# Replaying a fixed instruction order, banks and evacuating engines in place of a greedy planner: attention with memory, gated feed-forward, one core

## The chip, the cores and the metric

The kernel runs on one core of one Trainium2 chip. Five engines work side by side: TensorE (PE in the profile, its weight loads PEld), VectorE (DVE), ScalarE (ACT), GpSimd (POOL) and SyncE (SP), which here only issues DMAs. Each engine carries out its own instructions in order and waits on semaphores for those of the others. The metric is the device time of one launch in microseconds; lower is better.

## The reference

Two branches are computed from the same 2048 x 512 input and mixed per token by a sigmoid gate. Branch A is attention with 32 heads of width 16 in four segments of 512 tokens, plus a read of a running memory M, z of the segments before. Branch B is a feed-forward block of width 1792 with a ReLU gate. Cut to what matters:

```python
for s in range(4):
    logits = einsum('bhqd,bhkd->bhqk', qs, ks) * scale + mask   # causal inside the segment
    a_dot = einsum('bhqk,bhkd->bhqd', softmax(logits), vs)
    num = einsum('bhld,bhde->bhle', phi(qs), M)
    den = einsum('bhld,bhd->bhl', phi(qs), z)[..., None] + 1e-06
    outs.append(g * num / den + (1.0 - g) * a_dot)              # g = sigmoid(beta), per head
    M = M + einsum('bhld,bhle->bhde', phi(ks), vs)
    z = z + einsum('bhld->bhd', phi(ks))
a = concat(outs) @ wo
b = (relu(x @ W_gate) * (x @ W_up)) @ W_down
out = sig * a + (1 - sig) * b                                   # sig = sigmoid(sum(x * gate_w))
```

All inputs and the output are bfloat16.

## The kernel before

The kernel is a small planner and an emitter. `program` (from L619 on) walks through the computation and makes one `Op` for each group of instructions: its engine or engines, its code, the names that it reads and writes, and for work in PSUM an `Epoch`, the holder of a bank. `Sched.add` numbers the operations and works out what each depends on. `Sched.run` then places them one by one with a model of their durations, `Sched.place` notes which semaphores each has to wait for, and `Sched.emit` writes the five engines' programs. Nothing of the planning is left at run time: what the chip sees are five fixed instruction lists with waits.

The work of each segment s:

- **Projections** (`proj`). q and k by head group of 128 columns (four groups G), v by token tile: 16 products each of 128 x 128 weights on 512 columns. An evacuation casts each PSUM bank to SBUF (`qcp`, `kcp`, `vcp`; DVE or ACT), and two masks of k (`kmask`) write `kp`, in which the two heads of a pair stand apart. For the first segment's q, `step = 1 if early else 2` makes every product an operation of its own, and the list is then put in order by contraction tile.
- **Attention** (`att`). 18 visits: `visit` makes a "quad" (L912), four row tiles of 32 that fill four PSUM banks at once, an exponential over 2048 columns on ACT (L928) into `E`, and on POOL the causal masks (L934). After the visits of a head group, `flush` makes its PV block (L968, 64 matmuls on two banks), two transposes on DVE that empty the banks (`tr`, L978), and a chain `rden`, `rdg`, `ad`, `bt`, `oa` that divides, scales and turns the result into `oT`.
- **Memory** (`mu`, `nd`): an update of M (L835) and, from the second segment on, four readouts (L855).
- **Feed-forward** (`ffn`): 14 blocks f, each with 4 products for gate and 4 for up (L1042), a ReLU (`relu`, DVE or ACT) and a product with it (`hm`, DVE) into `hT`.
- **Output** (`outp`): per token tile 4 products with wo (L1074) and 14 with W_down (L1081) in one bank, a final scaling (`fin`) and a store. The last tile is split into 384 and 128 columns.
- **Gate** (`gate`): rows of x are loaded again (`ldxr`, L742) into the slots `osb`, multiplied and summed on DVE (L745). From the second segment on all rows use slot 2.

The x of the first segment is loaded plainly (`ldhT`) and turned by PE against the identity (L706, `xt`), with eight copies (`xc`) on DVE and ACT. Ahead of it PE runs warm-up products on constants (L692). The weights follow on SP, all loads of the first half of gate and up (`ldwg0`, `ldwu0`), then the second half (`ldwg1`, `ldwu1`).

The order is made greedily: for each engine there are queues with priorities; `ready` says from when an operation may start by the model, `_choose` takes one, with a jitter and other settings drawn from a seed for every 8 us of planned time; `_bank_choice` picks PSUM banks, 0 to 3 for the visits and mostly 4 to 7 for the rest; an evacuation that may run on DVE or ACT goes to whichever takes it first. `DCOST`, `LAND0` and `landing` say how long loads take.

Of the kernel before, what the change touches and what calls it, by code (L numbers as in the profile page):

```python
# [2 lines left out]

# [13 lines left out]
LAG = 0  # L17
PAIR = 1
LASTK = 17
HWAIT = 250.0  # L20
HEARLY = 3500.0
MWAIT = 500.0
PVR = 2
NEXT = 1150.0
TNN = 2
STRICT = 6000.0
PE_LAT = 175.0
SWITCH = 106.0
GATE_T = {0: 20000.0, 1: 44000.0, 2: 90000.0, 3: 140000.0}
UNIT_T = 400.0  # L30
X1_T = 19000.0
X2_T = 34000.0
H1_T = 14000.0
LX = 300.0
DCOST = {"ldwg0_0": 1000.0, "ldbraw": 1800.0, "ldgwb": 1300.0, "ldx1_0": 1500.0, "vsh0": 1100.0, "vsh1": 1100.0, "vsh2": 1100.0, "vsh3": 1100.0}
LAND0 = {"ldhT0": 2850.0, "ldhT2": 3100.0, "ldwq0": 3150.0, "ldwq1": 3200.0, "ldwq2": 3100.0, "ldwq3": 3000.0}
NBLK = 36
QTN, EKN, HTN, OTN, XR = 8, 4, 19, 8, 3
SBX = 0
LOW_T = {"main": 0.0, "att": 3000.0, "proj": 2000.0, "ffn": 2000.0, "mid": 3000.0, "out": 5000.0}  # L40
WIN = 8000.0
EVAC_P = 0.5
ND_P = 0.2
ADP = 1
TSP = 0
OAP = 0
UNITS = [[8] * 18] * 4
ORDER = [[(0, 1, 7, 2, 6, 3, 5, 4), (4, 0, 1, 7, 2, 6, 3, 5)] * 2] * 4
# [30 lines left out]
class Epoch:  # L79
    _n = 0  # L80

    def __init__(self, cls="mid", nb=1, at=None):
        self.nb = nb
        self.at = at
        self.group = (self,)
        Epoch._n += 1
        self.res = f"ACCep{Epoch._n}"
        self.bank = None
        self.readers = []
        self.cls = cls  # L90


class Op:
    __slots__ = ("engs", "eng", "fns", "occs", "lat", "reads", "writes", "name", "dma", "nbytes", "mode", "ep", "role",
                 "after", "nbk", "port", "base", "preds", "stream", "idx", "start", "end", "done", "cidx", "gate", "nd", "mates")

    def __init__(self, alts, reads=(), writes=(), name="", lat=0.0, dma=False, nbytes=0, mode="f", ep=None, role=None):
# [13 lines left out]
        self.after = 0.0  # L111
        self.nbk = 2
        self.port = name.startswith(PORT)
        self.base = None
        self.preds = []
        self.gate = None
        self.mates = ()
# [11 lines left out]
class Sched:  # L129
    ENGS = ("pe", "act", "dve", "pool", "sp")  # L130
    CAPS = {"ffn": 3, "proj": 2, "mid": 2, "out": 2}

    def __init__(self, ndma=16, nbanks=8, seeds=(0,)):
        self.seeds = seeds
        self.jit = {}
        self.knobs = {}
        self.low_from = False
        self.mates = ()
# [9 lines left out]
        self.queues = {e: [] for e in self.ENGS}  # L148
        self.dma_rr = 0
        self.port_free = 0.0  # L150
        self.relax = False
# [7 lines left out]
        self.busy = {e: 0.0 for e in self.ENGS}  # L159
        self.ops = []  # L160
        self.log = []
# [8 lines left out]
    def add(self, op):  # L170
# [42 lines left out]
        self.ops.append(op)  # L213
        return op

    def queue(self, prio, ops):
        by = {}
        for t in ops:
            for e in t.engs:
                by.setdefault(e, []).append(t)  # L220
        for e, ts in by.items():
            self.queues[e].append([prio, ts, 0])

    def _bank_free(self, prev, e):
        if prev is None:
            return 0.0
        return max((r.end + LAT for r in prev.readers if self.know[e][r.stream] < r.idx), default=0.0)

    def pv_due(self):
        q = self.queues["pe"][self.pvq]  # L230
        while q[2] < len(q[1]) and q[1][q[2]].done:
            q[2] += 1
        if q[2] >= len(q[1]) or q[1][q[2]].gate is None:
            return 0
        t = self.now["pe"] + 500.0
        return (PVR if q[1][q[2]].mates else q[1][q[2]].nbk) if all(p.done and p.end <= t for p, _ in q[1][q[2]].preds) else 0

    def next_visit(self):
        q = self.queues["pe"][self.attq]
        while q[2] < len(q[1]) and q[1][q[2]].done:  # L240
            q[2] += 1
        return q[1][q[2]] if q[2] < len(q[1]) else None

    def visit_in(self, dt):
        op = self.next_visit()
        if op is None:
            return False
        t = self.now["pe"] + dt
        if op.after > t or not all(p.done and p.end <= t for p, _ in op.preds):
            return False  # L250
        return all(p.done and p.end <= t + 700.0 for g in op.ep.group for rd in g.readers for p, _ in rd.preds if p.ep not in op.ep.group and p.cidx < op.cidx)

    def soon(self, dt):
        op = self.next_visit()
        if op is None or op.after - HEARLY > self.now["pe"] + dt:
            return False
        if not all(p.done and p.end + LAT <= self.now["pe"] + dt for p, _ in op.preds):
            return False
        t = max((self._bank_free(x, "pe") if x is None or all(r.done for r in x.readers) else 1e9) for x in self.bank_ep[:4])
        return t <= self.now["pe"] + dt  # L260

    def next_sides(self):
        op = self.next_visit()
        return 0 if op is None else len(op.ep.group) - 1

    def low(self, cls):
        return 0 if self.low_from and (self.relax or not self.visit_in(LOW_T[cls])) else 4

    def _bank_choice(self, ep, e, taken=()):
        cls, nb, n = ep.cls, ep.nb, len(self.bank_ep)  # L270
        idle = [i not in taken and (p is None or all(r.done for r in p.readers)) for i, p in enumerate(self.bank_ep)]
        if ep.at is not None:
            own = range(ep.at, ep.at + nb)
            return (ep.at, max(self._bank_free(self.bank_ep[i], e) for i in own)) if all(idle[i] for i in own) else None
        lo = 4 if cls == "side" else self.low(cls)
        if cls in ("proj", "ffn", "mid", "out"):
            held = sum(not f and p.cls == cls for f, p in zip(idle, self.bank_ep))
            if held + nb > (self.knob()[3] if cls == "ffn" else 2):
                return None
            free = sum(idle[lo:])  # L280
            if (free - nb < max(self.pv_due(), 1) if nb == 1 else free < (2 if self.relax else 3)):
                return None
            room = sum(idle[4:]) - (self.next_sides() if self.visit_in(self.knob()[1]) and not self.relax else 0)
        else:
            room = 8
        best = None
        for bi in range(lo, n - nb + 1):
            if not all(idle[bi:bi + nb]) or bi + nb > 4 and min(nb, bi + nb - 4) > room:
                continue
            ft = max(self._bank_free(p, e) for p in self.bank_ep[bi:bi + nb])  # L290
            key = ft + (300.0 if bi < 4 else 0.0)
            if nb == 1:
                key += 0.0 if not idle[bi ^ 1] else 200.0
            if best is None or key < best[2]:
                best = (bi, ft, key)
        return best and best[:2]

    def _banks(self, op, e):
        taken, out, t = set(), [], 0.0
        for ep in op.ep.group:  # L300
            bc = self._bank_choice(ep, e, taken)
            if bc is None:
                return None
            out.append((ep, bc[0]))
            taken |= set(range(bc[0], bc[0] + ep.nb))
            t = max(t, bc[1])
        return out, t

    def _pred_done(self, op, e):
# [5 lines left out]
    def ready(self, op, e):  # L315
        t0 = self.now[e]
        t = op.after - (HEARLY if op.mode == "r" and self.mode == "h" else 0.0)
        if op.gate is not None:
            if self.mode != "r" and not self.relax and not (op.gate.done and self.now["pe"] > op.gate.start + STRICT) and not (op.gate.done and (self.next_visit() is None or self.soon(NEXT))):
                return None  # L320
            for m in op.mates:
                for p in self._pred_done(m, e):
                    if p.eng != "pe":
                        if not p.done:
                            return None
                        t = max(t, p.end + LAT - 900.0)
            lo = self.low("att")
            ft = sorted(self._bank_free(p, e) for p in self.bank_ep[lo:] if p is None or all(r.done for r in p.readers))
            if len(ft) < op.nbk:
                return None  # L330
            t = max(t, ft[op.nbk - 1])
        for p in self._pred_done(op, e):
            if not p.done:
                return None
            if self.know[e][p.stream] < p.idx:
                t = max(t, p.end + LAT)
        if op.ep is not None:
            if op.role == "w" and op.ep.bank is None:
                for rd in [x for g in op.ep.group for x in g.readers]:
                    for p, _ in rd.preds:  # L340
                        if p.ep in op.ep.group or p.cidx > op.cidx:
                            continue
# [121 lines left out]
    def _choose(self, e):  # L464
# [28 lines left out]
        if not heads:  # L493
            return None
# [707 lines left out]
```

## Time and profile before

| | us |
|---|---|
| median of 3 runs | 263.42 |
| lowest, highest | 262.78, 263.67 |
| profiled execution, its own time | 263.54 |
| its span, first to last instruction | 262.3 |

The profile page says for each engine how long it was busy; the view of the chain follows the work back from the last instruction and names what each step waited for. A row of a timeline begins with its start and its length in us; in rows of groups the number behind the bar is the busy time in us and then the mean length of one in ns. A PE row's length includes the drain of the array, so consecutive matmuls overlap: the distance of two starts is what one costs.

### The profile page before, as it was taken

What the parts mean: (1) busy time and instruction counts of PE and PEld (TensorE: products, weight loads), DVE (VectorE), ACT (ScalarE), POOL (GpSimd) and SP (SyncE); (2) the same over time, 40 slices, a digit from 0 to 9 for tenths busy, and PEclk for the clock granted to TensorE, in tenths of its full rate; (3) what the DMA queues carried; (4) which work ended last, traced back from release to release, by engine and by line L of the source; (5) the groups of instructions that cost most, each with busy time, mean ns of one, the idle gap of its engine ahead of it and who ended that gap; (6) DMA issues with size and microseconds to landing.
All of it is one profiled execution on the core that took longest, in us unless ns stands there. A gap on an engine that the chain in (4) does not pass through costs nothing.

```text
span 262.3 us, 6420 instructions
## 1 busy us (share of the span) xinstructions
PE 255.7 (97%) x2619; PEld 114.7 (44%) x2653; DVE 179.5 (68%) x356; ACT 184.5 (70%) x160; POOL 130.7 (50%) x295
## 2 busy tenths in 40 slices
PE   8999999999999999999999999999999999999997
PEld 5444443444344544434444544444444444444444
DVE  5488878788986577778788577757667716467600
ACT  4586689999789779785778687677777665576021
POOL 3036557564646457666645457846364454545100
PEclk9999999999999999999999999999999999999999
DMA  6999746930261135212040232010132100100011
GB/s 200 290 308 249 162 63 135 287 46 22 66 143 40 24 74 109 62 23 24 19 107 7 56 96 27 2 41 2 22 82 43 23 21 22 40 2 2 0 42 40
DMA packets 34925, 19.87 MB, mean 76 GB/s; under 512 B 24016, under 2 KB 34128, under 8 KB 34896
## 3 DMA queue, kind: packets, MB, share of 16 engines
q1 hardware_dynamic: 34800, 19.46, 31.6%
q8 instruction: 21, 0.34, 0.6%
q14 instruction: 8, 0.07, 0.1%
q10 hardware_dynamic: 96, 0.00, 0.0%
HBM read 10.40 MB, written 2.11 MB: 48 GB/s over the span
## 4 chain that ended last, share of the span: by engine, by line
PE 97%; issue 1%; DVE 1%
PE ps L1042 38%; PE ps L1081 19%; PE ps L792 11%; PE ps L912 9%; PE ps L968 6%; PE ps L790 5%; PE ps L1074 5%; PE ps L855 1%; PE ps L692 1%; PE ps L706 1%; PE ps L835 0%; DVE hT L1053 0%; DVE Tn L978 0%; DVE osb L745 0%; DVE osb L1090 0%
## 5 line engine op out<-in xcount | busy, mean ns | idle before, releaser
L934 POOL TENSOR_SCALAR_AFFINE_SELECT E<-E 64x256 bf16<-64x256 bf16 (+1 forms) x256 | 110.3, 442 | 112.2 <-ACT E L928 82.9
L928 ACT ACTIVATE E<-ps 128x2048 bf16<-128x2048 f32 x72 | 135.1, 1876 | 38.7 <-PE ps L912 38.6
L1042 PE MATMUL ps<-xT,wu 128*128 128x512 bf16 x213 | 57.2, 380 | 1.4 <-issue 1.3
L1042 PE MATMUL ps<-xT,wg 128*128 128x512 bf16 x219 | 57.7, 380 | 0.6 <-issue 0.3
L1081 PE MATMUL ps<-wd,hT 128*128 128x512 bf16 (+2 forms) x229 | 52.8, 367 | 0.9 <-issue 0.6
L1053 DVE TENSOR_TENSOR hT<-ps,rl 128x512 bf16<-128x512 f32 x56 | 38.5, 687 | 16.6 <-PE ps L1042 16.4
L1081 PEld LDWEIGHTS ps<-wd,hT 128*128 128x128 bf16 x238 | 21.4, 98 | 23.8 <-issue 2.4
L1042 PEld LDWEIGHTS ps<-xT,wg 128*128 128x128 bf16 x224 | 20.6, 98 | 25.7 <-issue 2.8
L1042 PEld LDWEIGHTS ps<-xT,wu 128*128 128x128 bf16 x224 | 20.1, 98 | 25.4 <-issue 3.5
L912 PE MATMUL ps<-qT,kp 32*128 32x192 bf16 (+7 forms) x512 | 28.6, 287 | 0.0
L978 DVE STREAM_TRANSPOSE Tn<-ps 128x512 f32<-128x512 f32 x32 | 21.3, 696 | 8.7 <-PE ps L968 8.7
L1051 DVE TENSOR_SCALAR rl<-ps 128x512 bf16<-128x512 f32 x30 | 20.7, 690 | 8.5 <-PE ps L1042 8.2
L1090 DVE TENSOR_SCALAR osb<-ps,omg 128x512 bf16<-128x512 f32 (+1 forms) x8 | 5.6, 701 | 26.0 <-PE ps L1081 15.1
L1050 ACT ACTIVATE rl<-ps 128x512 bf16<-128x512 f32 x26 | 15.5, 598 | 10.0 <-PE ps L1042 9.7
L912 PEld LDWEIGHTS ps<-qT,kp 32*128 32x128 bf16 x512 | 8.2, 92 | 25.3 <-issue 13.1
L968 PE MATMUL ps<-E,vaug 64*17 64x128 bf16 (+7 forms) x512 | 18.7, 283 | 0.0
L968 PE MATMUL ps<-E,vsh 64*17 64x128 bf16 (+7 forms) x512 | 18.3, 283 | 0.0
L1091 ACT ACTIVATE osb<-ps,omg 128x512 bf16<-128x512 f32 (+1 forms) x9 | 6.1, 674 | 16.4 <-PE ps L1074 14.0
L792 PE MATMUL ps<-xT,wq 128*128 128x512 bf16 x61 | 16.0, 390 | 0.4 <-issue 0.3
L1074 PE MATMUL ps<-wo,oT 128*128 128x512 bf16 (+2 forms) x67 | 16.2, 366 | 0.2 <-issue 0.2
L792 PE MATMUL ps<-xT,wk 128*128 128x512 bf16 x60 | 15.6, 380 | 0.4 <-issue 0.3
L968 PEld LDWEIGHTS ps<-E,vaug 64*17 64x17 bf16 x512 | 11.6, 86 | 8.5 <-issue 4.4
(68 smaller groups left out, 233.6 us busy)
## 6 DMA issues: line engine op xcount, KB each, us to landing
vsh<-vaug SPq DMA_DIRECT2D x8, 272.0 KB, 4.2
osb<-in_A_x_dram SPq DMA_DIRECT2D x16, 128.0 KB, 2.3
out_dram<-osb SPq DMA_DIRECT2D x15, 128.0 KB, 1.7
wg<-in_B_W_gate_dram SPq DMA_DIRECT2D x8, 224.0 KB, 5.7
wu<-in_B_W_up_dram SPq DMA_DIRECT2D x8, 224.0 KB, 6.2
wd<-in_B_W_down_dram SPq DMA_DIRECT2D x1, 1792.0 KB, 10.6
hT<-in_A_x_dram SPq DMA_DIRECT2D x2, 256.0 KB, 2.9
wq<-in_A_wq_dram SPq DMA_DIRECT2D x4, 128.0 KB, 3.5
```

Of the source, the lines that this page charges most:

```text
L792: ins = e.matmul(A(ep)[:, :], lhsT=w[:, kt, col * 128:(col + 1) * 128], rhs=V.xT[:, kt, tok:tok + 512], start=(kt == 0), stop=(kt == KT - 1))
L912: ins = q.matmul(dst, lhsT=V.kp[r, kslot(s, G), c, :], rhs=V.qT[r, qslot(s, G), q0:q0 + w], start=True, stop=True, tile_position=(32 * jj, ...
L928: acts.append(act(lambda a: a.activation(V.E[:, base * 512:base * 512 + min(2048, 4 * W)], PF[:, 0:min(2048, 4 * W)], ACT.Exp, scale=SCALE ...
L934: pools.append(pool(lambda g, ap=ap, lim=lim, pat=pat: g.affine_select(out=ap, in_=ap, compare_op=ALU.is_ge, fill=0.0, base=lim, pattern=[ ...
L968: ins = q.matmul(A(eps[p])[32 * jj:32 * jj + 17, 64 * (c + u):64 * (c + u + n)], lhsT=v[:, 8 * G + 2 * jj + p, :], rhs=V.E[r, f:f + 64 * n ...
L978: ds.append(dve(lambda e, p=p, ep=eps[p]: e.transpose(V.Tn[:, 2 * (G % (TNN // 2)) + p, :], A(ep)[:, :]), t_dve(512), writes=[f"Tn{2 * (G ...
L1042: ins = e.matmul(A(ep)[:, :], lhsT=w[:, kt, f * 128:(f + 1) * 128], rhs=V.xT[:, kt, c % XR * 512:(c % XR + 1) * 512], start=(kt == 0), sto ...
L1050: evs.append(sc.add(Op([("act", lambda e, ep=eg, r=r: e.activation(V.rl[:, r, :], A(ep)[:, :], ACT.Relu), t_act(512)), ("dve", lambda e, e ...
L1051: ("dve", lambda e, ep=eg, r=r: e.tensor_scalar(V.rl[:, r, :], A(ep)[:, :], 0.0, None, ALU.max), t_dve(512))],
L1053: evs.append(dve(lambda e, ep=eu, r=r, hs=hs: e.tensor_tensor(V.hT[:, hs, :], A(ep)[:, :], V.rl[:, r, :], ALU.mult), t_dve(512), reads=[f" ...
L1074: ins = e.matmul(A(ep)[:, 0:c1 - c0], lhsT=V.oT[:, ot[G], i * 128:(i + 1) * 128], rhs=V.wo[:, G, c0:c1], start=st_ and G == 0, stop=sp_ an ...
L1081: ins = e.matmul(A(ep)[:, 0:c1 - c0], lhsT=V.hT[:, slots[f], i * 128:(i + 1) * 128], rhs=V.wd[:, f, c0:c1], start=st_ and f == f0, stop=sp ...
```

## The change

The planning by priorities, seeds and jitter goes. In its place stand three tables: `ORDER`, for each engine the numbers of its operations in the order of issue; with it, for operations that could run on DVE or on ACT, the engine in whose list they stand; and `BANKS`, one digit for each epoch. `run` gives the epochs their banks and places the operations in the order of the tables; waits are made as before, by `place` and `_waits`. Beside this:

- The DVE's four clears of PSUM banks 4 to 7 (`init`, L684) and the waits for them are gone; the warm-up and the transposes of x take banks from the table.
- The three small loads on ACT (`touch`) stand ahead of the first activation, which brings ACT's function table.
- The copies of the turned x are on DVE and ACT in turn; the transposes run in the order of the two halves.
- `visit` can take parts of several quads (`SEVEN`); all its lists are empty, so each visit is one quad with four banks as before. The first bank is taken from the table and is not always 0.
- The output's product with wo no longer waits for W_down and hT.
- Constants of the model of landing times are different.

```diff
-    sc = Sched(seeds=(237719, 74891, 0, 89398, ...))
+    sc = Sched(ORDER, BANKS)
...
+SEVEN = [(), (), (), ()]
+BANKS = ("616534605734265415767000000670001567000007610045556456654754664764575476764067744547060574754566600000560000476000004500"
...
+ORDER = {k: [int(x) for x in v.split()] for k, v in {
+    "pe": """
+57 58 59 61 63 65 67 69 71 73 133 143 158 159 134 160 135 161 136 148 138 149 139 173 144 174 192 163 193 164 195 189 145 190 146 186 187 384 385 201
...
+    "act": """
+0 1 2 3 62 66 70 74 162 140 153 194 196 178 188 202 400 75 208 185 214 220 406 418 226 237 340 243 89 334 249 335 342 255 448 272 350 278 343 358 284
...
+    "dve": """
+56 60 64 68 72 137 150 142 141 175 176 165 154 191 155 147 388 152 179 394 180 76 401 151 79 395 172 84 86 412 389 413 82 407 424 425 77 166 419 95
...
+    "sp": """
+4 5 6 7 8 9 10 11 12 13 14 15 16 17 18 19 20 21 22 23 24 25 27 83 44 81 26 85 157 35 28 36 37 29 39 38 200 94 199 30 31 33 156 87 182 34 181 32 96 45
...
     def run(self):
+        for ep in self.eps:
+            if ep.at is None:
+                ep.bank = int(self.banks[ep.idx])
+            else:
+                ep.bank = ep.at
+        todo = {e: [self.ops[i] for i in self.order[e]] for e in self.ENGS}
+        assert sorted(i for e in self.ENGS for i in self.order[e]) == list(range(len(self.ops)))
+        at = dict.fromkeys(self.ENGS, 0)
         while True:
...
+            heads = [(e, todo[e][at[e]]) for e in self.ENGS if at[e] < len(todo[e])]
+            if not heads:
+                return
+            cands = [(t, self.ENGS.index(e), e, op) for e, op in heads for t in (self.start_of(op, e),) if t is not None]
+            assert cands, [(e, op.name) for e, op in heads]
             start, _, e, op = min(cands, key=lambda c: c[:2])
             self.place(op, e, start)
-            self.relax = False
+            at[e] += 1
...
+    def start_of(self, op, e):
+        t = 0.0
+        for p in self._preds(op, e):
             if not p.done:
                 return None
+            t = max(t, p.end + LAT)
+        if op.ep is not None and op.role == "w":
+            for p in self._holders(op):
+                for r in p.readers:
+                    if not r.done:
+                        return None
+                    t = max(t, r.end + LAT)
...
-    for b in range(4):
-        ds.append(dve(lambda e, b=b: e.memset(PS[:, 4 + b, :], 0.0), 500, writes=[f"init{b}"], name=f"init{b}"))
...
-    for h, kt, bank, eng in ((0, 0, 0, "dve"), (0, 1, 1, "act"), (0, 2, 2, "act"), (1, 0, None, "dve"), (0, 3, 3, "dve"), (1, 1, 0, "act"), (1, 2, 1, "dve"), (1, 3, 2, "act")):
-        ep = Epoch("att") if bank is None else None
...
+    for h, kt, eng in ((0, 0, "dve"), (0, 1, "act"), (0, 2, "dve"), (0, 3, "act"), (1, 0, "dve"), (1, 1, "act"), (1, 2, "dve"), (1, 3, "act")):
+        ep = Epoch("att")
...
-        if s == 0:
-            qp = [[p for p in pes if p.name == f"q0_{col}"] for col in range(4)]
-            pes = [qp[col][kt] for kt in range(4) for col in range(4)] + [p for k in "kv" for p in pes if p.name[0] == k]
```

The numbers of the tables are the places of the operations in the order in which `program` makes them. Put into names (`.0`, `.1` are the parts of one bank's products, `quad`s end in the number of the visit), the stretches that matter here read:

```text
PE    warm warm xt0 .. xt7 | q0_0.0 q0_1.0 q0_2.0 q0_2.1 q0_0.1 q0_2.2 q0_0.2 q0_2.3 q0_0.3 k0_1.0 k0_0.0 k0_1.1 k0_0.1 k0_3.0
      q0_1.1 k0_3.1 v0_3.0 k0_2.0 v0_3.1 k0_2.1 quad0_0_0 v0_2.0 q0_1.2 ...
      ... pv0_0 quad0_1_7 q1_0.0 q1_1.0 q1_0.1 q1_1.1 wg0_9.0 wg0_9.1 quad0_1_8 wg0_7.0 wg0_8.0 k1_0.0 wg0_7.1 wg0_8.1 k1_0.1 wu0_8.0 ...
DVE   pm xc0 xc2 xc4 xc6 qcp0_0 ... vone hm0_1 qcp0_3 gate1 gate2 relu0_4 hm0_0 hm0_4 gate0 hm0_3 relu0_6 hm0_6 reb kmask0_2_0
      hm0_5 gate4 tr0_0_0 tr0_0_1 gate3 qcp1_0 ...
SP    ldhT0 ldhT2 ldwq0-3 ldwk0-3 ldwv0-3 ldwg0_0-3 ldwu0_0-3 ldbraw ldxr1 ldx2_2 ldxr0 ldgwb ldxr2 kT20_1 ldwu1_3 ldwg1_0 ldx1_0
      ldx1_1 ldwg1_1 ldx1_3 ldx1_2 vsh0_1 ldxr4 vsh0_0 ldwg1_2 ldwg1_3 ldwu1_1 kT20_0 ldxr3 kT20_3 ldwu1_2 kT20_2 ldwu1_0 ldxr5 ...
      grd0 ldx2_0 ldxr6 ldxr7 ldwd ...
```

More of the change, by code (lines that the diff above doesn't have):

```diff
@@ L87, in __init__ @@
         self.res = f"ACCep{Epoch._n}"
[L88 removed]
+        self.bank = self.idx = None
         self.readers = []
@@ L213, in add @@
         self.ops.append(op)
-        return op
[L216 to L309, printed above, removed]
+        for x in () if op.ep is None else op.ep.group if op.role == "w" else (op.ep,):
+            if x.idx is None:
+                x.idx = len(self.eps)
+                self.eps.append(x)
@@ L313, in _pred_done, with _holders @@
             yield p
[L315 to L332, printed above, removed]
+    def _holders(self, op):
+        return {id(p): p for ep in op.ep.group for p in self.bank_ep[ep.bank:ep.bank + ep.nb] if p is not None}.values()
+    def start_of(self, op, e):
+        t = 0.0
+        for p in self._preds(op, e):
             if not p.done:
                 return None
[L335 to L342, printed above, removed]
-                        if not p.done:
-                            return None
-                        t = max(t, p.end - op.occs["pe"] - (3000.0 if op.ep.cls == "out" else 300.0))
-                bc = self._banks(op, e)
-                if bc is None:
-                    return None
-                t = max(t, bc[1])
-            elif op.ep.bank is None:
-                return None
+            t = max(t, p.end + LAT)
[5 more added lines that the diff above has]
+                    t = max(t, r.end + LAT)
         if e == "pe" and t > 0:
@@ L747, in program @@
-        gq["act"].append(act(lambda e, t0=t0, t1=t1, gx=gx: e.activation(gx, V.gl[:, t0:t1], ACT.Exp), 215, reads=[f"gl{t}" for t in range(t0, t1)], writes=[f"gexp{c}"], name="gexp"))
+            dma("sp", lambda e, t=t, row=row: e.dma_start(row, A_x[0, t * 128:(t + 1) * 128, :]), 1 << 17, writes=rows, name=f"ldxr{t}")
+            dve(lambda e, t=t, row=row: e.tensor_tensor_reduce(out=row, in0=row, in1=V.gwb[:], scale=1.0, scalar=0.0, op0=ALU.mult, op1=ALU.add, accum_out=V.gl[:, t:t + 1]),
+                                 775, reads=rows + ["gwb"], writes=rows + [f"gl{t}"], name=f"gate{t}")
@@ L936, in visit @@
-            vres[vid] = [f"E{base + j}" for j in range(nb)] + [f"V{vid}m{lim}_{i}" for lim in (0, 64) for i in range(len(runs))]
+                for o, j, ep, i, G, c, q0, w in todo:
+                    r = slice(-32 * j, 32 - 32 * j)
+                    ins = q.matmul(PS[:, ep.bank + i, o:o + w], lhsT=V.kp[r, kslot(s, G), c, :], rhs=V.qT[r, qslot(s, G), q0:q0 + w], start=True, stop=True, tile_position=(-32 * j, 0), skip_group_check=True)
+                return ins
+            W = max(x[0][1] for x in pieces)
```

609 lines of the change are left out of this document (192 added, 417 removed), and 34 rows, old and new, of the table ORDER.

## The prediction

> **What bounds the kernel now.** I read the page first: the engines' busy shares, then the chain that ended last.
>
> ```profile
> span 262.3 us, 6420 instructions
> ...
> PE 255.7 (97%) x2619; PEld 114.7 (44%) x2653; DVE 179.5 (68%) x356; ACT 184.5 (70%) x160; POOL 130.7 (50%) x295
> ...
> PE 97%; issue 1%; DVE 1%
> ```
>
> TensorE is busy for 97% of the span and holds 97% of the chain. A busy PE need not be a PE at its peak, so the second view is what it waited for in all:
>
> ```profile
> PE ps L1042 <- issue: 1.6, 10, 0.2
> PE ps L692 <- PEq L1187: 0.8, 1, 0.8
> PE ps L1081 <- issue: 0.6, 4, 0.2
> PE ps L792 <- issue: 0.6, 4, 0.2
> ...
> PE ps L1042 <- DVE Tn L978: 0.2, 1, 0.2
> ```
>
> Apart from the start (0.8 us) there is one wait of 0.2 us for another engine. The eighteen "issue" waits of at most 0.2 us, 2.8 us together, may not be idle at all: each is as long as one missing matmul record, as the third view, PE's timeline around two attention visits, lets one check.
>
> ```profile
> 233.31 0.81 PE L1042 MATMUL ps<-xT,wu 128*128 128x512 bf16 x3 [0.16 <-issue]
> ...
> 236.21 0.40 PE L912 MATMUL ps<-qT,kp 32*128 32x384 bf16 x8
> 236.54 0.60 PE L1042 MATMUL ps<-xT,wg 128*128 128x512 bf16 x2
> 236.98 1.03 PE L1042 MATMUL ps<-xT,wu 128*128 128x512 bf16 x4
> 237.84 1.03 PE L1042 MATMUL ps<-xT,wg 128*128 128x512 bf16 x4
> ...
> 239.67 0.40 PE L912 MATMUL ps<-qT,kp 32*128 32x320 bf16 x8
> ...
> 244.49 1.10 PE ps L968 x64
> ```
>
> Four 512-column products take 0.86 us (from 236.98 to 237.84), so 0.216 each. From 236.54 to 239.67 there are 14, 3.02 us; 0.11 us more pass before the next visit starts. A visit with the change back costs 0.33 us (236.21 to 236.54), of which its own columns are 0.21. So one stay in the row-tiled attention work costs about 0.11 + 0.12 = 0.23 us beside its columns, and nothing else is lost here. (The last row is from the chain: a PV block, 1.10 us.) At 233.31 a group is x3 where its neighbours are x4, with 0.16 us "idle" before it: the missing record.
>
> The last views are the two ends.
>
> ```profile
> 3.74 1.89 PE L706 MATMUL ps<-ident,hT 128*128 128x128 bf16 x16
> 5.42 4.17 PE L792 MATMUL ps<-xT,wq 128*128 128x512 bf16 x16
> 12.55 0.40 PE L912 MATMUL ps<-qT,kp 32*128 32x512 bf16 x4
> ...
> 5.39 0.18 PEld L792 LDWEIGHTS ps<-xT,wq 128*128 128x128 bf16 x2
> 5.85 0.15 PEld L792 LDWEIGHTS ps<-xT,wq 128*128 128x128 bf16 x1 [0.28 <-issue]
> 6.28 0.15 PEld L792 LDWEIGHTS ps<-xT,wq 128*128 128x128 bf16 x1 [0.28 <-issue]
> ...
> 260.02 0.39 PE L1074 MATMUL ps<-wo,oT 128*128 128x128 bf16 x4
> 260.45 0.35 DVE L1090 TENSOR_SCALAR osb<-ps,omg 128x128 bf16<-128x128 f32 x1 [10.86 <-PE ps L1074]
> ...
> out_dram<-osb SPq DMA_DIRECT2D x1, 32.0 KB, 1.5
> ```
>
> The first useful product waits for the first load of x to land (3.74); the first two q products are 0.43 us apart (5.42 to 5.85 to 6.28), half rate; after them 0.216 holds to the end. Behind the last product (260.41) lie one evacuation and one 32 KB store: 1.9 us. From 3.74 to 260.41 PE is a sum of fixed pieces. The run's own time is 263.54, 1.24 above its span, and 0.12 above the median 263.42.
>
> **The change, part by part.** *PE's work.* Both orders have 946 products of the full-width kind (928 for q, k, v, gate, up and output, plus 18 as the last tile is split), 72 visits, 16 PV blocks, 12 memory readouts and 3 memory updates; nothing is added. What an order can change is how often PE enters the tiled work. In the trace before there are 73 such stays, from the quad at 12.55 to the PV at 244.49. Decoding the PE table into names and counting gives 73 too. 73 - 73 = 0 stays of 0.23 us: 0.0 us. Which kind follows which inside a stay differs a little (three memory updates now stand ahead of a quad, not behind one): at most 0.05 us each, -0.15 to +0.15.
>
> On that price the Trainium skill, TensorEngine Tiling (Array Packing), Key Properties, says that changing the tiling mode drains the array. Had the table scattered the 16 PV blocks into stays of their own, the sum would have been up to 16 x 0.23 = 3.7 us worse; the count says that it doesn't.
>
> *The four q products in single steps.* `step = 1 if early else 2` stands in the kernel before already, and its order ran them contraction tile by contraction tile. The table's first ones are q0_0, q0_1, q0_2 of tile 0, then tiles 1 to 3 of q0_2 and q0_0, then k; most of q0_1 and q0_3 comes after the first visit. 30 products stand before the first visit in both. Worth 0.0.
>
> *The transposes of x ahead.* The fifth transposed pair is now the one that q0_0 needs (it was the fourth).
>
> ```profile
> 4.17 0.43 DVE L713 CAST xT<-ps 128x256 bf16<-128x256 f32 x1 [1.02 <-PE ps L706]
> 4.82 1.09 DVE L713 CAST xT<-ps 128x256 bf16<-128x256 f32 x3 [0.21 <-PE ps L706]
> 4.39 0.66 ACT L713 ACTIVATE xT<-ps 128x256 bf16<-128x256 f32 x2 [2.08 <-PE ps L706]
> ```
>
> A pair takes 2 x 0.107 us, and the first copy starts 0.43 us after its pair. The fifth pair starts at 3.74 + 4 x 0.213 = 4.59, its copy at 5.02, ends at 5.02 + 0.43 = 5.45, against 5.39 when PE was free: +0.06 us (0 to +0.2). The three touch loads now stand ahead of ACT's table load; ACT's first copy has until 4.39, so this is covered; uncovered, its copies would be late by what three issues take, some 1.3 us. The four clears of PSUM that go were DVE's, done before 4.17: 0.0.
>
> *Engines of the evacuations.* Counting the tables against the trace: ACT gets 6 masks of k and 4 casts more and 2 final scalings less; DVE the reverse, and no clears.
>
> ```profile
> L818 DVE CAST vaug<-ps 128x512 bf16<-128x512 f32 x12 | 8.3, 691 | 2.7 <-PE ps L790 2.7
> L809 DVE TENSOR_SCALAR kp<-kT,pm 128x512 bf16<-128x512 bf16 x25 | 8.7, 359 | 2.6 <-ACT kT L797 1.9 <-PE ps L912 0.7
> L810 ACT ACTIVATE kp<-kT,pm 128x512 bf16<-128x512 bf16 x7 | 5.0, 720 | 0.0
> L797 ACT ACTIVATE vaug<-ps 128x512 bf16<-128x512 f32 x4 | 2.4, 599 | 1.4 <-PE ps L790 1.4
> L1091 ACT ACTIVATE osb<-ps,omg 128x512 bf16<-128x512 f32 (+1 forms) x9 | 6.1, 674 | 16.4 <-PE ps L1074 14.0 <-PE ps L1081 2.4
> L928 ACT ACTIVATE E<-ps 128x2048 bf16<-128x2048 f32 x72 | 135.1, 1876 | 38.7 <-PE ps L912 38.6
> 46.00:60.00 14.00, 13.79 (x143) 5.96 (x144) 11.12 (x22) 13.36 (x12) 8.60 (x18) 1.00 0.69 164
> ```
>
> ACT: 6 x 0.720 + 4 x 0.599 - 2 x 0.674 = +5.4 us, to 189.9, 72% of the span; DVE falls. No bound changes over the whole, but one stage is tight: from 46 to 60 us ACT was busy for 13.36 of 14 us, and PE still had no gap. In the tables the worst six visits in a row (from the ninth on) hold 19.6 us of ACT work by these rows in 19.8 us of PE work; the worst six of the kernel before (from the seventh on) held 18.8 in 18.5. The shortest distance of two visits is 10 products in both, 10 x 0.216 + 0.44 = 2.6 us, with 1.88 for the exponential between. Cost 0.0, with up to +0.8 should ACT fall behind there.
>
> *Loads.* SP's table moves the second halves of gate and up (8 x 224 KB) behind other loads, and the x rows for the gate forward. Entry ldxr4 refills the row that gate2 has read, so SP stands until gate2 is done. On DVE that comes behind qcp0_3, which reads the 68th product: 5.4 + 0.4 + 68 x 0.216 + 4 x 0.44 = 22.3, then 0.7 for the cast and 2 x 0.84 for gate1 and gate2, with the latencies between some 25.1. Behind ldxr4 are vsh0, the last loads of gate and up, and the k transposes.
>
> ```profile
> 1.72 1.85 SPq L618 DMA_DIRECT2D wq<-in_A_wq_dram  x4
> ...
> 16.82 1.24 SPq L620 DMA_TRANSPOSE xT<-in_A_x_dram  x1
> wu<-in_B_W_up_dram SPq DMA_DIRECT2D x8, 224.0 KB, 6.2
> DMA to landing us min/median/max: 2.0/2.3/9.7
> L745 DVE CUSTOM_DVE_ANT_0 osb<-osb,gwb 128x512 bf16<-128x512 bf16 x16 | 12.2, 760 | 1.1 <-DMA osb<-in_A_x_dram 1.1
> L978 DVE STREAM_TRANSPOSE Tn<-ps 128x512 f32<-128x512 f32 x32 | 21.3, 696 | 8.7 <-PE ps L968 8.7
> ```
>
> (The row of the landing times is that of the x rows, L742.) The last weight load, ldwu1_0, is ten issues later: six loads at 0.46, three transposes at 1.25 and one vsh, for which I put 0.6: 25.1 + 7.1 = 32.2. With 6.2 us it lands at 38.4. Its first reader, wu0_8, is the 133rd product: 5.4 + 0.4 + 132 x 0.216 + 9 visits and a PV (4.1) + nine changes into them (1.0) = 39.4. Covered by 1.0 us: 0.0; at the 9.7 us of the slowest x row, 2.5 us late.
>
> **Sum**, against the profiled 263.54: 0.0 for the stays, +0.06 for the start, 0.0 for evacuations and loads: 263.6; against the median 0.12 lower. I forecast **263.5**, no change. About 0.3% (0.8 us) is what can be told from no change here.
>
> **Rivals.**
>
> *Slower: gate4 ahead of the first PV's evacuation.* On DVE, gate4 (which needs ldxr4) stands directly ahead of the two transposes that empty pv0_0's banks, and wg0_9, a visit and eight products later, takes the first of these banks. pv0_0 ends at 5.4 + 0.4 + 108 x 0.216 + 7 x 0.33 + 8 x 0.11 + 1.1 (a PV, by the row at 244.49) = 33.4. PE has 0.33 + 8 x 0.216 to do before wg0_9, so it is there at 35.5. Behind ldxr4, issued at 25.1, come gate4 (0.84 with its read of the accumulator) and a transpose (0.70): a landing time over 35.5 - 25.1 - 1.5 = 8.9 us decides. At the 9.7 us that the slowest such load took, the transpose ends at 34.8 + 1.5 = 36.3; PE stands for 0.8 us, and about 0.4 more at the next bank behind the same DVE queue: 264.7. Against it: the median is 2.3, and the 9.7 lay behind the load of W_down, which now comes later.
>
> *Slower: ACT falls behind from 36 to 80 us.* For it: 19.6 of 19.8. If its work there takes 4% more than the rows say, the six visits lose 0.6 us, and their neighbours (43.9 us in 47.6 over fourteen visits) some 0.2: 264.3. Against it: 18.8 in 18.5 before cost PE nothing, as slack carries over from visit to visit.
>
> *Faster: the "issue" waits were real.* Then an order without them could win up to 2.8 us, half of it 262.1. Against: each stands at a group one record short.
>
> *The change does nothing of what its words on q say*: the steps were single before; same time as the forecast.
>
> *Slower: half rate for longer.* If all 16 q products ran at the 0.43 us of the first two, 14 x 0.211 = 3.0 us more; at four more, 0.8: 264.4. The trace shows two; the runs lie within 0.9 us.
>
> The Trainium skill, TensorE: Matmul & The Clock Gate, Part 1, says that full rate comes after a busy window of about 3.4 us which runs free of the kernel's start, so the number of slow products varies by run; the trace has the step about 5.5 us after PE's first product, and shows one run only.
>
> **Chances and range.** Forecast with the q rival 0.66; gate4 0.10; ACT 0.11; half rate 0.04; faster 0.09. The three slower ones come to 264.3 to 264.7, 0.3% up and more; a little of the forecast spills over the bound on both sides. Faster 0.11, same 0.63, slower 0.26. The forecast alone spans 262.9 to 264.1 (runs of before: 262.78 to 263.67); up to the ACT and most of the gate4 case the range is 262.7 to 264.7.
>
> **What would show it.** Right: PE busy near 97%, the second q product 0.43 after the first, 73 stays, last product near 260.4. Wrong: a wait of PE on Tn (L978's successor) near 35 us; on qT or E between 36 and 80; or a PE sum that is shorter with the same count of stays, which I could not explain.

## The result and the profile after

The changed kernel takes 264.24 us (median of 6 runs, 263.88 to 264.52) against 263.21 us for the kernel before beside it (262.78 to 263.67). The ratio is 1.0037, with a 95% interval of 1.0024 to 1.0049: slower by about 1.0 us. Measured again later it was 263.96 against 263.35, ratio 1.0033 (1.0020 to 1.0045). The ratios here and below are those on record; they are not the quotients of the medians (263.96 / 263.35 is 1.0023), and the two can differ by 0.1%. The profiled execution of after took 264.29 us, that of before 263.54.

The page of after: the span, the engines' busy shares, and the shares of the chain that ended last.

```profile
span 263.0 us, 6414 instructions
...
PE 259.3 (99%) x2653; PEld 114.2 (43%) x2653; DVE 172.0 (65%) x344; ACT 189.1 (72%) x168; POOL 120.7 (46%) x295
...
PE 96%; DMA 2%; SPq 1%; issue 0%; DVE 0%
```

PE rose from 97% to 99% only because all 2653 matmul records are there this time (2619 before), and with them the "issue" share is gone. New in the chain are DMA and SPq, 3% together. All that PE waited for, from the view of waits (line, what it waited for, us in total, times, longest):

```profile
PE ps L502 <- PEq L903: 0.8, 1, 0.8
PE ps L576 <- DMA wk<-in_A_wk_dram: 0.5, 1, 0.5
```

The second row is new: one wait of a projection for the load of wk. PE's timeline of after shows where (start, length, then the instructions), and the timeline of its weight loads shows the whole of it.

```profile
3.60 1.90 PE L511 MATMUL ps<-ident,hT 128*128 128x128 bf16 x16
5.54 2.10 PE L576 MATMUL ps<-xT,wq 128*128 128x512 bf16 x9
8.16 2.33 PE L576 MATMUL ps<-xT,wk 128*128 128x512 bf16 x10 [0.52 <-DMA wk<-in_A_wk_dram]
...
12.80 0.40 PE L689 MATMUL ps<-qT,kp 32*128 32x512 bf16 x4
```

```profile
5.51 1.64 PEld L576 LDWEIGHTS ps<-xT,wq 128*128 128x128 bf16 x9 [0.27 <-DVE xT L518]
8.16 0.55 PEld L576 LDWEIGHTS ps<-xT,wk 128*128 128x128 bf16 x4 [1.01 <-DMA wk<-in_A_wk_dram]
```

Nine q products run at 0.216 us each from 5.54, which takes them to 7.48; then PE stands until 8.16, 0.68 us by starts (the row's 0.52 begins at the modelled end of the last product). The kernel before had sixteen q products there, and the k products' weights were asked for only at 9.22:

```profile
9.22 0.74 PEld L792 LDWEIGHTS ps<-xT,wk 128*128 128x128 bf16 x4
```

The landing times of the four wk loads from their issue at 3.6 to 5.0 us, first in before, then in after:

```profile
DMA to landing us min/median/max: 3.1/3.2/3.3
```

```profile
DMA to landing us min/median/max: 3.4/3.9/4.0
```

The first k operation is two products, which read wk's first two tiles, and it waits for both. The second tile landed at 7.42 before and at 8.11 after. Before, it had 1.8 us to spare. The other end of after, in its timeline and in the view of the DMAs from 260.3 us on (queue and kind: packets, MB, share; then the issues with KB each and us to landing):

```profile
260.29 0.39 PE L845 MATMUL ps<-wo,oT 128*128 128x128 bf16 x4
260.71 0.35 DVE L860 TENSOR_SCALAR osb<-ps,omg 128x128 bf16<-128x128 f32 x1 [7.90 <-PE ps L845]
```

```profile
q14 instruction: 1, 0.01, 0.8%
...
out_dram<-osb SPq DMA_DIRECT2D x1, 96.0 KB, 1.6
out_dram<-osb SPq DMA_DIRECT2D x1, 32.0 KB, 1.9
```

The last store takes 1.9 us where it took 1.5, and one packet of instructions moves beside it. By the trace the packet has 8192 bytes, starts at 261.88 (the store was issued at 261.09) and takes 0.49 us.

Between the two ends nothing changed: from the first visit to the last products there are 247.47 us in before (12.55 to 260.02) and 247.49 in after (12.80 to 260.29). So, profile against profile, +0.25 at the start, +0.02 between, +0.48 for the store (1.96 against 1.48 from its issue to the end of the span), 0.75 in all, and 264.29 - 263.54 = 0.75.

### The profile page after: what moved, and what is told of

Same layout as the page of the kernel before. It is cut to its first block, busy times and chain, and to the rows that moved or that the text cites. A ratio compares the mean times of both kernels' runs of the same rounds, so it can differ in the third digit from the quotient of the medians.

```text
span 263.0 us, 6414 instructions
## 1 busy us (share of the span) xinstructions
PE 259.3 (99%) x2653; PEld 114.2 (43%) x2653; DVE 172.0 (65%) x344; ACT 189.1 (72%) x168; POOL 120.7 (46%) x295
## 4 chain that ended last, share of the span: by engine, by line
PE 96%; DMA 2%; SPq 1%; issue 0%; DVE 0%
PE ps L815 38%; PE ps L852 19%; PE ps L576 10%; PE ps L689 9%; PE ps L736 7%; PE ps L574 5%; PE ps L845 5%; DMA wk<-in_A_wk_dram 2%; PE ps L632 1%; SPq L448 1%; PE ps L615 1%; DVE osb L860 0%
## 5 line engine op out<-in xcount | busy, mean ns | idle before, releaser
L706 POOL TENSOR_SCALAR_AFFINE_SELECT E<-E 128x256 bf16<-128x256 bf16 (+1 forms) x256 | 100.8, 420 | 111.4 <-ACT E L699 102.0
L815 PE MATMUL ps<-xT,wu 128*128 128x512 bf16 x224 | 61.3, 380 | 0.0
L815 PE MATMUL ps<-xT,wg 128*128 128x512 bf16 x224 | 60.6, 380 | 0.0
L852 PE MATMUL ps<-wd,hT 128*128 128x512 bf16 (+2 forms) x238 | 57.1, 367 | 0.0
L576 PE MATMUL ps<-xT,wk 128*128 128x512 bf16 x64 | 18.2, 379 | 0.5 <-DMA wk<-in_A_wk_dram 0.5
L576 PE MATMUL ps<-xT,wq 128*128 128x512 bf16 x64 | 18.1, 380 | 0.0
L574 PE MATMUL ps<-wv,xT 128*128 128x512 bf16 x64 | 18.0, 380 | 0.0
L753 POOL TENSOR_TENSOR adT<-Tn,rdg 128x512 bf16<-128x512 f32 x12 | 12.7, 1055 | 11.1 <-DVE rdg L751 10.7
L860 DVE TENSOR_SCALAR osb<-ps,omg 128x512 bf16<-128x512 f32 (+1 forms) x10 | 7.0, 706 | 14.6 <-PE ps L845 7.9
```

The costliest lines, as they stand in the source:

```text
L574: ins = e.matmul(A(ep)[:, :], lhsT=V.xT[:, kt, tok + col * 128:tok + (col + 1) * 128], rhs=w[:, kt, :], start=(kt == 0), stop=(kt == KT - 1))
L576: ins = e.matmul(A(ep)[:, :], lhsT=w[:, kt, col * 128:(col + 1) * 128], rhs=V.xT[:, kt, tok:tok + 512], start=(kt == 0), stop=(kt == KT - 1))
L706: pool(lambda g, ap=ap, lim=lim: g.affine_select(out=ap, in_=ap, compare_op=ALU.is_ge, fill=0.0, base=lim, pattern=[[0, 4], [1, 64]], chan ...
L815: ins = e.matmul(A(ep)[:, :], lhsT=w[:, kt, f * 128:(f + 1) * 128], rhs=V.xT[:, kt, c % XR * 512:(c % XR + 1) * 512], start=(kt == 0), sto ...
L852: ins = e.matmul(A(ep)[:, 0:c1 - c0], lhsT=V.hT[:, slots[f], i * 128:(i + 1) * 128], rhs=V.wd[:, f, c0:c1], start=st_ and f == f0, stop=sp ...
```

## The experiments

| run | what it is | us, median | kernel before beside it | ratio (95%) |
|---|---|---|---|---|
| e1 | after, SP's stream longer | 264.04 | 263.18 | 1.0031 (1.0017 to 1.0046) |
| e2 | after, 12 q products ahead of k | 263.76 | 263.18 | 1.0021 (1.0010 to 1.0032) |
| e3 | e1 and e2 | 263.74 | 263.18 | 1.0023 (1.0013 to 1.0034) |
| f1 | after's code, orders of before | 263.30 | 263.18 | 1.0011 (0.9997 to 1.0024) |
| e4 | after, POOL's stream longer | 263.84 | 263.12 | 1.0024 (1.0015 to 1.0033) |
| e5 | after, ScalarE's stream longer | 263.44 | 263.12 | 1.0012 (1.0003 to 1.0021) |
| e7 | e2 and e5 | 263.03 | 263.55 | 0.9989 (0.9978 to 0.9999) |
| f2 | f1, ScalarE's stream longer | 264.11 | 263.55 | 1.0022 (1.0012 to 1.0032) |
| g1 | after again | 263.96 | 263.35 | 1.0033 (1.0020 to 1.0045) |
| g2 | e7 again | 262.97 | 263.35 | 0.9990 (0.9981 to 0.9999) |
| g3 | e5 again | 263.38 | 263.35 | 1.0001 (0.9992 to 1.0010) |

The kernel before moves by 0.4 us between groups, so differences below are taken inside a group, or by the ratios.

**f1: is it the orders at all?** The tables of after are overwritten with the order, engines and banks of before, but for two copies of x, which the new code ties to the other engine.

```diff
-BANKS = ("616534605734265415767000000670001567000007610045556456654754...
+BANKS = "3012340125041657467540000007600004460000046000547657546754...
...
-ORDER = {k: [int(x) for x in v.split()] for k, v in {
-    "pe": """57 58 59 61 63 65 67 69 71 73 133 143 158 159 134 160 135 161 136 148 ...
+ORDER = {k: [int(x) for x in v.split()] for k, v in {
+    "pe": """57 58 59 61 63 67 65 69 71 73 133 143 158 168 134 144 159 169 135 145 160 170 136 146 161 171 138 ...
```

> The code of after with orders, engines and banks of the kernel before written into its tables (two evacuations of x swapped between VectorE and ScalarE, since the code now fixes their engine; the four q products of the second output tile stand together as before). If the time is lost by the orders alone: 16 q products ahead of k, no wait for wk, no fetch beside the last store unless SP's instructions happen to end there, 263.2. If the code besides the tables costs the time (touches ahead of the table load, the PSUM clears, the waits): 264.0 to 264.3.

It took 263.30. PE's timeline of f1, and its last store in the view of the DMAs:

```profile
3.78 1.34 PE L509 MATMUL ps<-ident,hT 128*128 128x128 bf16 x14
5.43 0.28 PE L509 MATMUL ps<-ident,hT 128*128 128x128 bf16 x2 [0.31 <-DVE xT L516]
5.55 3.62 PE L574 MATMUL ps<-xT,wq 128*128 128x512 bf16 x16
9.01 3.19 PE L574 MATMUL ps<-xT,wk 128*128 128x512 bf16 x13
```

```profile
out_dram<-osb SPq DMA_DIRECT2D x1, 32.0 KB, 1.5
```

No wait for wk, no fetch at the end, and the time of before to within the error. The clears, touches and waits of the new code cost nothing that can be told (the interval allows 0.6 us at most); the loss is in the tables.

**e1: whose instructions are fetched?** My first theory was that they are SP's, since SP is the only engine still issuing at 261.9.

```diff
                         res = op.fns[e](engobj)
+                        if e == "sp" and op.name == "ldwd":
+                            for _ in range(12):
+                                engobj.wait_ge(self.sem["pe"], 1)
```

> Twelve waits that have long been met are added on SP behind the issue of the wd load at 51.7 us, where SP then idles until 66.9 us, so that SP's instruction stream is 12 instructions further along at the end. Theory (an 8192-byte instruction fetch of SP, which began at 261.88 us in the run after, 0.79 us behind the issue of the last store, holds one DMA engine for 494 ns and with it the last store): the fetch moves to well ahead of the end, the last store lands about 1.46 us after its issue as before and not 1.94, and the time is 264.24 - 0.48 = about 263.8. Rival (the five last stores are issued within 4.1 us instead of 8.4 us, and the last one queues behind the others): the landing stays at 1.94 us and the time at 264.2.

The view of the DMAs of e1 from 260.3 on:

```profile
q14 instruction: 1, 0.01, 1.0%
...
out_dram<-osb SPq DMA_DIRECT2D x1, 32.0 KB, 2.1
```

The fetch stayed and the time too, 264.04. Two waits share one instruction, so SP's stream grew by six and not by twelve. But the fetch, which began with SP's 141st record in after, begins with its 147th here: it does not go by SP's count.

**e2 and e3: the wait for wk.** In e2 three more of q's single steps stand ahead of k; e3 adds the waits of e1.

```diff
+def move(eng, ids, behind=None, ahead=None):
+    o = ORDER[eng]
+    for i in ids:
+        o.remove(i)
+    k = o.index(ahead) if behind is None else o.index(behind) + 1
+    o[k:k] = ids
+
+move("pe", [144, 145, 146], ahead=148)      # q0_1.1 to q0_1.3, ahead of k0_1.0
```

> On PE the single steps 1, 2 and 3 of q's second output tile are put ahead of the first k product, so that 12 q products stand there instead of 9. Theory (PE stood 0.5 to 0.7 us ahead of the first k product for the landing of wk's second tile, because the single steps had taken seven q products from in front of it): three products of 0.216 us fill that gap, the wait falls from 0.52 to under 0.1 us, the last product starts about 0.5 us earlier, at 259.7 to 259.8 us, and the time is about 263.7. Rival (the start is not what moved the end; the 0.25 us that the first visit is late is given back or is lost again behind it): the last product stays at 260.2 to 260.3 us and the time at 264.2.

> The twelve SP waits and the three q products ahead of k in one kernel. If the two causes are the whole of the slowdown and independent, the gains add up: 264.24 - 0.48 - 0.5 = about 263.2 to 263.3, level with the kernel before (263.2). If either is a story, the time stays at 263.7 or above.

e2 took 263.76 and its last products start at 259.67 (260.29 in after), about as the theory had it. e3 did not add up, 263.74 and not 263.2: its fetch is still there (at 260.89), and 2.25 us pass from its last store's issue to the end. So one part of the loss was explained, and the fetch was still without an owner.

**e4 and e5: POOL or ScalarE.** By the records of the traces, ScalarE's stream has 175 instructions before and 189 after, POOL's 345 and 312 (the expectations count one or two more). The fetches on this queue have 8192 bytes each, and three of them lie at the same places of VectorE's stream in both profiles: behind its 61st, 192nd and 315th record in before, its 64th, 194th and 317th in after, so about 128 apart. One of the others starts behind the 61st to 63rd record of ScalarE in each profile (72.7 us in before, 65.9 in after); 62 + 128 = 190, at the end of a stream of 189, which a stream of 175 never reaches. POOL's fit as well by its records (181 + 128 = 309), so both were tried. The two edits differ in their first line only; both first lines are shown, with the run behind the #:

```diff
+                        if e == "pool" and op.name == "pm8c":         # e4
+                        if e == "act" and op.name == "relu3_12":      # e5
+                            for _ in range(24):
+                                engobj.wait_ge(self.sem["pe"], 1)
```

> The 8192-byte instruction fetch stayed beside the last store with SP's stream moved on, so it is not SP's. Two other engines have a stream that ends where a fetch would fall, if fetches come every 128 instructions: POOL (313 instructions; fetches behind about its 55th and 181st, the next about its 312th) and ScalarE (191 instructions; a fetch behind its 62nd, the next about its 190th). Here POOL gets 24 more waits that have long been met (12 instructions) at its idle start. Theory POOL: the fetch moves to about 12 POOL instructions earlier, 239 to 243 us, the last store lands 1.48 us after its issue, and the time is 264.2 - 0.5 to 0.7 = 263.6 to 263.7. Theory ScalarE (rival): the fetch stays about 0.8 us behind the last store's issue, and the time at 264.0 to 264.2.

> The same with ScalarE: 24 waits that have long been met (12 instructions) behind the relu at 243 us, where ScalarE then idles until 255.4 us. Theory ScalarE: its second fetch falls at 243 to 256 us, the last store lands 1.48 us after its issue, and the time is 263.6 to 263.7. Theory POOL (rival): the fetch stays beside the last store, and the time at 264.0 to 264.2.

The DMAs from 260.3 us on, first in e4, then in e5:

```profile
q14 instruction: 1, 0.01, 0.8%
...
out_dram<-osb SPq DMA_DIRECT2D x1, 32.0 KB, 2.0
```

```profile
out_dram<-osb SPq DMA_DIRECT2D x1, 96.0 KB, 1.6
out_dram<-osb SPq DMA_DIRECT2D x1, 32.0 KB, 1.5
```

and in e5 between 244 and 246 us:

```profile
q14 instruction: 1, 0.01, 1.5%
```

With twelve instructions more on ScalarE the fetch goes to 244.72 us, behind ScalarE's 193rd record, and the span ends 1.47 us after the store's issue again, for 263.44. With twelve more on POOL it stays, and e4 has a ninth fetch instead, at 231.05 us behind POOL's 310th record: POOL's refill is another one. The fetch at the end is ScalarE's. (e4's 263.84 lies 0.2 to 0.3 us below after by the ratios, inside their error; no run shows a cause for that.)

**f2: the other way round.** Fourteen instructions that do nothing, put on ScalarE in f1 (28 waits behind `relu3_13`), make its stream 189 long.

> The old orders in the tables of after (263.30) with 28 waits that have long been met behind the relu at 242.4 us on ScalarE, which then idles until 251.3 us: its stream becomes 191 instructions, as long as in the kernel after. Theory (a fetch of ScalarE's next 128 instructions falls at the end of a stream of 191 and holds up the last store): an 8192-byte fetch appears 0.8 us behind the last store's issue, that store lands 1.95 to 2.25 us after its issue instead of 1.48, and the time is 263.30 + 0.5 to 0.7 = 263.8 to 264.0. Rival (the fetch beside the store came from the new orders, not from the length of ScalarE's stream): no fetch there, 263.3.

The page's row of the instruction queue in f1 and in f2, and f2's DMAs from 260.3 us on:

```profile
q14 instruction: 8, 0.07, 0.1%
```

```profile
q14 instruction: 9, 0.07, 0.1%
```

```profile
q14 instruction: 1, 0.01, 0.8%
...
out_dram<-osb SPq DMA_DIRECT2D x1, 32.0 KB, 1.9
```

One fetch more, beside the store: from its issue to the end 1.95 us pass and not 1.48, 0.47 us more in the profile. The time is 264.11 where f1 took 263.30, but the kernel before was slower in that group too; the difference is 0.44 us by the medians, each against its own before, and 0.3 by the ratios (1.0022 against 1.0011), with intervals that overlap. So the length of ScalarE's stream alone brings the fetch to the end, also with the old orders; the price in time is better read from g1 and g3.

**e7, g1 to g3: both mended.** e7 has the edits of e2 and e5. g1 to g3 ran together, to split the loss on one chip.

> Three q products ahead of the first k product, and ScalarE's stream 12 instructions longer behind the relu at 243 us. Theory (the slowdown is the wait for wk's tile at the start and the fetch beside the last store, and nothing else): both are gone, the fetch falls at 243 to 256 us, the last store lands 1.48 us after its issue, and the time is 263.44 - 0.4 = 263.0 to 263.2, level with the kernel before. Rival (something else in the new orders costs time, as the run with three q products and SP waits, which came out at 263.74, would leave open): 263.4 or above.

> The kernel after, unchanged, on the same chip as the two runs beside it, since the kernel before has moved between 263.1 and 263.6 us from one chip and hour to the next. Expected 1.0 us above the kernel before, with a fetch beside the last store.

> Three q products ahead of k and the longer ScalarE stream, again. Theory (start and tail are the whole loss): 0.9 to 1.1 us below the kernel after beside it, 0 to 0.5 us below the kernel before. Rival (the first reading, 0.5 us below before, was the chip's drift): 0.3 us above before or more.

> The longer ScalarE stream alone, again. It splits the loss: 0.5 to 0.7 us below the kernel after (the fetch beside the last store) and 0.3 to 0.5 us above the run with both mended (the wait ahead of the k products). If it equals the run with both mended, the start is worth nothing.

263.96 with both faults, 263.38 with the fetch moved, 262.97 with the q products moved too: 0.58 us for the tail, 0.41 for the start, 0.99 together. The mended kernel is 0.38 us below the kernel before in that group and 0.52 in e7's by the medians, about 0.3 in both by the ratios: just faster, as both intervals end at 0.9999. PE's timeline of e7, then of g3:

```profile
5.36 3.10 PE L590 MATMUL ps<-xT,wq 128*128 128x512 bf16 x12
8.30 2.75 PE L590 MATMUL ps<-xT,wk 128*128 128x512 bf16 x12
...
12.71 0.40 PE L703 MATMUL ps<-qT,kp 32*128 32x512 bf16 x4
```

```profile
5.30 2.12 PE L579 MATMUL ps<-xT,wq 128*128 128x512 bf16 x9
7.63 2.51 PE L579 MATMUL ps<-xT,wk 128*128 128x512 bf16 x10 [0.21 <-DMA wk<-in_A_wk_dram]
...
12.45 0.40 PE L692 MATMUL ps<-qT,kp 32*128 32x512 bf16 x4
```

e7's first visit is later than g3's by 0.26 us, but 32 products stand ahead of it and not 30, which take 0.43 more; and one execution says little about the start. The thirteen profiles together say more. "Lost" is the start of the first visit, less that of the first q product, less 0.216 for each product between (30, or 32 with twelve q products ahead of k):

| q products ahead of k | kernel: lost, us | mean |
|---|---|---|
| 9 | after 0.78, e1 0.70, e4 0.55, e5 0.72, g1 0.47, g3 0.67 | 0.65 |
| 12 | e2 0.30, e3 0.09, e7 0.44, g2 0.59 | 0.36 |
| 16 | before 0.65, f1 0.09, f2 0.37 | 0.37 |

Two things are in it. The first q products ran at half rate, none in after and three in before; and wk's second tile landed between 6.90 us (f2) and 8.11 (after). The wait can also move on to the fourth tile (8.10 to 9.04), which the third k operation needs, four products behind the first: e4 stood there for 0.43 us. With nine ahead slow products and waits stand in for each other: e5 lost 0.63 on slow products and did not wait, after had no slow product and waited. With twelve or sixteen only the products at half rate are left, and some 0.1 us that e3 and f1 lose as well. Nine against twelve makes 0.29 us by these means, somewhat less than the 0.41 of the times. The number of slow products varied from none to four, which bears out the Trainium skill, TensorE: Matmul & The Clock Gate, Part 1, where it calls the count run-variable.

## Where the prediction held and where it failed

The forecast was 263.5, no change; it came out at 264.24, inside the range, but 1.0 us above the kernel before in the first group and 0.6 in the last by the medians, where 0.8 was to tell a change from none; the intervals of both leave no doubt that it is slower. That it lies inside the range is luck: the upper part of the range was there for gate4 and for ACT, neither of which happened, and the two losses that did happen, 0.99 us together, are not in the sum.

**What held.** 247.49 us between the ends against 247.47 leave no stay and no order in the middle to pay for, and both traces have 73 stays: "0.0 for the stays". The "issue" waits were missing records, as argued; that rival falls. gate4 did not come late: PE has no wait for Tn. ScalarE did not fall behind: it is busy for 189.1 us (189.9 was worked out), and in the tight stage of after,

```profile
46.00:60.00 14.00, 14.00 (x145) 5.98 (x144) 10.59 (x23) 12.62 (x12) 8.63 (x20) 1.00 0.46 150
```

it has 12.62 us in 14 (13.36 before) while PE is never idle. The half rate did not last longer. That the four clears were worth 0.0 is in line with f1.

**The step that failed at the start** is *The four q products in single steps*: "30 products stand before the first visit in both. Worth 0.0." The count is right and was the wrong count. What matters is how many stand before the first product that needs the next load: sixteen before, nine after. From the first q product at 5.42 nine products end at 7.36 at full rate, and at 7.92 with the 0.56 us that three products at half rate cost in that trace, while wk's second tile landed at 7.42. The margin fell from 1.8 us to between 0.5 and -0.1, less than one load's spread; the prediction timed the late loads (gate, up, x rows) and not these. Measured: +0.41 us, by g3 against g2.

**The step that failed at the end** is the fixed tail: "Behind the last product (260.41) lie one evacuation and one 32 KB store: 1.9 us", taken as unchanged. The move of evacuations to ScalarE was costed in busy time (+5.4 us, nothing on the path), not in instructions. Eight operations and six separate waits more made its stream 189 long instead of 175, and the refill that falls there holds the last store. Measured: +0.58 us, by g1 against g3.

**The start of the transposes** was to cost +0.06. In the three profiles with the old orders the first q product starts at 5.42, 5.55 and 5.69, in the ten with the new ones at 5.23 to 5.54, on the mean 0.18 us earlier. But 0.12 of that lies ahead of the transposes: the first of them starts at 3.71 on the mean with the old orders and at 3.59 with the new, as the first half of x landed earlier in those executions (3.49 against 3.66), and three profiles are few. Behind it the old orders need 1.84 us to the first q product and the new ones 1.78. In f1 the last transposed pair waits 0.31 us for a copy of x; no profile with the new orders has such a split before its last pair for that reason. So about 0.06 us may be a gain of the new orders; most of the 0.3 to 0.5 by which the mended kernel lies below before is not explained.

So by the medians of the last group the change loses 0.41 + 0.58 and gains some 0.4, of which the cause is open: 0.6 us slower (1.03 in the first group).

## What to carry to other kernels

When an order is changed at the start of a kernel bound by one engine, count for each load the work that stands ahead of its first reader, and take the landing time with its spread (here 1.2 us between executions of one load), not from one trace. When the end hangs on a small store, look at the last microsecond for DMAs that are not the kernel's own: here a stream that ended just at a refill point paid for it, and twelve idle instructions on that engine moved it away. Equal sums of engine work between two fixed points show at once that a loss is at the ends.

## What the runs showed of the hardware

An instruction refill during the run can hold up a store. The last store of 32 KB is 128 packets of 256 bytes in the trace. In each of the seven profiles with the fetch at the end (after, e1 to e4, f2, g1), exactly eight of them, as many as fall to one of the 16 DMA engines, wait for the fetch: the first starts at its end to within 0.01 us, and the others follow one behind the other; the last of the other 120 has started 0.2 to 0.7 us before:

| | fetch, start and ns | pause ahead of the last eight packets, us | from issue to the end, us |
|---|---|---|---|
| after | 261.88, 494 | 0.21 | 1.96 |
| e2 | 261.30, 916 | 0.66 | 2.25 |
| e5 | none | none | 1.47 |

Over all thirteen profiles the span ends 1.95 to 2.25 us after the store's issue with the fetch beside it and 1.47 to 1.48 without. The Trainium skill, DMA: Bandwidth & Descriptors, Queues, rings and completion order, says that a DMA engine goes round its queues packet by packet; a whole packet of 8192 bytes ahead of the store's eight is in line with that.

What starts the fetch at that moment stays open. ScalarE's last operation ended at 260.29 in after, 1.6 us earlier; in all seven profiles the fetch begins within 0.05 us of the start of SP's next to last closing wait.
